# Filter tables in full rows spread on chip, multiplies off GpSimd, and a larger filter piece in a spectral and feed-forward mix on one core

## The chip, the cores and the metric

The kernel runs on one core of a Trainium2 chip. The metric is the device time of one execution in microseconds (us). Beside timed runs there is one execution taken with the hardware profiler, whose trace gives start and length of each instruction. TensorE (PE) multiplies matrices, VectorE (DVE) and ScalarE (ACT) work on elements and read TensorE's results from PSUM, GpSimd (POOL) is a further engine for element work in SBUF, and SyncE (SP) issues most DMA transfers, in the order of its queue.

## The reference

```python
# x: (1, 2048, 512) bf16; w_r, w_i: (2048, 257) bf16; w1: (512, 1792); w2: (1792, 512)
g = sigmoid((x * gate_w).sum(-1, keepdims=True))
X = jnp.fft.rfft2(x.astype(jnp.float32), axes=(-2, -1))
a = jnp.fft.irfft2(X * (w_r + 1j * w_i), s=(2048, 512), axes=(-2, -1)).astype(jnp.bfloat16)
h = jnp.einsum("bsd,df->bsf", x, w1) + b1
sp = jnp.log1p(jnp.exp(-jnp.abs(h))) + jnp.where(h > 0, h, 0)
b = jnp.einsum("bsf,fd->bsd", h * jnp.tanh(sp), w2)
out = g * a + (1 - g) * b
```

The spectral half filters x in the frequency domain with a complex table; the feed-forward half is two matmuls with mish between them; a gate per row mixes them.

## The kernel before

Everything stays in SBUF, in large regions that are used several times (rA to rF, rW, rX). The spectral half goes through matmul steps over 16 tiles of x or 64 frequencies. Sums and differences of x (the butterflies `bf`, L648) go to rB; step `p` (L662, evacuated by `ep`) and step `d` (L673, evacuated by `ed` to rD) transform along rows and columns; y1 is written to a DRAM scratch in four parts (`s1w`) and read back in another layout as In in rE (`s1r`). Step `t` (L757) multiplies In with the constants M in eight groups q, and the evacuation `et` writes Y. The filter is then, for each group, the product of Y with the real table (`p1`, L772), the product of Y with its two halves of partitions exchanged (two DMA transfers `sa` and `sb` into a buffer z, one of three) with the imaginary table (`p2`, L775), and their sum (`ad`, L778). When all groups are done, the edge step (`e1`, L794, to `e3`) corrects one column. Step `it` (L830) with the constants G and step `id` (L869) transform back, with evacuations `eit` and `ey`; `ip` and `fin` bring the result to the output.

The feed-forward half works on four chunks of 512 rows: `mm1` (L890) takes x transposed (xT) and w1, `h` adds the bias (VectorE L897 or ScalarE L901 and L902), ScalarE applies exp, ln and tanh (L911 to L914), `mul` (L923) multiplies h with tanh in eight pieces a chunk, `mm2` (L939) multiplies with w2, and `o` (L953 or L956) scales by the gate. xT of tiles 0 to 3 is made by TensorE (`tr`, L635), that of tiles 4 to 15 by DMA transposes (L518).

The tables: for each of w_r and w_i the columns 0 to 128 are loaded straight into their place (`d` loads) and the columns 128 to 256 into a staging region in rA (`s` loads), each with three transfers, one of them over rows in reversed order. GpSimd copies the staged part column-reversed into the table (`rev`, L725, 32x2064 each, four a table). The real table is then copied to the other 64 partitions by a DMA (`wru`), the imaginary one negated to them by VectorE (L735).

What runs when is set before the launch: `_Graph.schedule` places each task by ready time, by the priority of its class in the table `KN`, and by an assumed cost of each engine, and so chooses the engine (GpSimd or VectorE for `mul`, p1, p2, ad; VectorE or ScalarE for evacuations). Each engine then executes its list strictly in order and waits on semaphores. TensorE's results go through three pairs of PSUM banks (pool `pr`) and two single ones (`mm2`).

Of the kernel before, what the change touches and what calls it, by code (L numbers as in the profile page):

```python
# [160 lines left out]
class _Task:  # L161
    __slots__ = ("name", "eng", "dur", "fn", "deps", "base", "sem", "semval", "idx", "sig", "start", "done",
                 "succ", "bl", "cls", "off", "prio", "xfer", "opts", "isdma", "bufs", "tab", "lat", "dur0")

# [862 lines left out]
```

## Time and profile before

| | us |
|---|---|
| median of 2 timed runs (lowest, highest) | 170.19 (169.14, 171.25) |
| the profiled execution | 170.5 |
| its span, first to last instruction | 168.8 |
| mean granted TensorE clock | 0.949 of full speed |
| chain that ended last, largest shares | VectorE 30%, SyncE's queue 24%, TensorE 20%, DMA 12% |
| first `t` matmul, first edge matmul | 86.27, 123.93 |

Times inside the span count from its first instruction. A row that groups instructions gives their number after an x; "idle before" is the time in which the engine stood still ahead of them, and the arrow names what ended it. A clock of 1.00 is 2.4 GHz and 0.50 is 1.2 GHz.

### The profile page before, as it was taken

The numbers are of one execution on the slowest core, as the hardware profiler recorded it, in microseconds if no ns is written. First come the engines' busy times: TensorE is split into PE (matmuls) and PEld (weight loads), VectorE is DVE, ScalarE is ACT, GpSimd is POOL, SyncE is SP. The second block draws the span as 40 slices with busy tenths as digits, with TensorE's granted clock in tenths as the row PEclk, the third lists the DMA queues.
The fourth block names the chain that finished last, engine by engine and source line by source line (L and its number), as shares of the span: only waits on it lengthen the run. The fifth ranks groups of instructions, "written<-read, shape, count | busy, mean of one in ns | idle before, by whom it ended". The sixth has DMA issues, their size and how long they took to land.

```text
span 168.8 us, 2313 instructions
## 1 busy us (share of the span) xinstructions
PE 134.8 (80%) x901; PEld 72.9 (43%) x901; DVE 138.3 (82%) x155; ACT 110.5 (65%) x75; POOL 58.8 (35%) x48
## 2 busy tenths in 40 slices
PE   4599999989108999857369969997058999999993
PEld 3454444574103565322136624342025658753362
DVE  1394846699995389399978999999997999999993
ACT  3337899999501999954369889699129999940000
POOL 3005000002995013997501547768900000390000
PEclk9999999999955799999999999999957999999999
DMA  5999546999999979999915525040000000000544
GB/s 134 331 396 243 116 70 154 357 116 101 102 159 396 294 190 243 118 250 371 402 52 130 132 62 124 14 108 9 0 0 0 0 4 0 0 0 0 188 162 153
DMA packets 31055, 23.98 MB, mean 142 GB/s; under 512 B 23940, under 2 KB 27908, under 8 KB 30596
## 3 DMA queue, kind: packets, MB, share of 16 engines
q1 hardware_dynamic: 30720, 23.60, 60.4%
q10 hardware_dynamic: 324, 0.23, 0.6%
q8 instruction: 7, 0.11, 0.3%
q14 instruction: 4, 0.03, 0.1%
HBM read 14.90 MB, written 4.19 MB: 113 GB/s over the span
## 4 chain that ended last, share of the span: by engine, by line
DVE 30%; SPq 24%; PE 20%; DMA 12%; issue 7%; POOL 5%; DVEq 0%; POOLq 0%
SPq L519 12%; PE ps L939 12%; SPq L518 12%; DMA rW<-rW 6%; DMA rW<-in_A_w_r_dram 5%; DVE tmp L775 5%; POOL rC L725 5%; DVE rA L772 4%; DVE hs L923 4%; DVE hs L897 4%; DVE rC L556 3%; PE ps L869 3%; DVE rA L778 2%; PE ps L830 2%; DVE rC L735 2%
## 5 line engine op out<-in xcount | busy, mean ns | idle before, releaser
L890 PE MATMUL ps<-rX,w_sb 128*128 128x512 bf16 x224 | 49.8, 379 | 6.2 <-DVE rD L897 3.8
L939 PE MATMUL ps<-w_sb,hs 128*128 128x512 bf16 (+1 forms) x182 | 42.0, 380 | 11.0 <-POOL hs L923 8.4
L890 PEld LDWEIGHTS ps<-rX,w_sb 128*128 128x128 bf16 x224 | 21.5, 98 | 32.5 <-DVE rD L897 4.3
L939 PEld LDWEIGHTS ps<-w_sb,hs 128*128 128x128 bf16 x182 | 17.7, 101 | 30.0 <-POOL hs L923 8.6
L897 DVE TENSOR_TENSOR hs<-ps,b1f 128x1024 bf16<-128x1024 f32 x16 | 19.2, 1217 | 8.4 <-PE ps L890 8.4
L914 ACT ACTIVATE uT<-uT 128x4096 bf16<-128x4096 bf16 (+1 forms) x8 | 25.5, 3190 | 0.1
L913 ACT ACTIVATE uT<-uT 128x4096 bf16<-128x4096 bf16 (+1 forms) x8 | 25.5, 3190 | 0.1
L923 POOL TENSOR_TENSOR hs<-hs,uT 128x768 bf16<-128x768 bf16 (+1 forms) x8 | 15.0, 1877 | 24.3 <-ACT uT L914 23.4
L911 ACT ACTIVATE uT<-hs 128x2048 bf16<-128x2048 bf16 (+1 forms) x12 | 20.3, 1695 | 2.8 <-DVE hs L897 1.8
L923 DVE TENSOR_TENSOR hs<-hs,uT 128x1024 bf16<-128x1024 bf16 (+1 forms) x16 | 19.8, 1294 | 2.8 <-ACT uT L914 2.8
L556 DVE CAST rC<-ps 128x1024 bf16<-128x1024 f32 x16 | 19.3, 1261 | 0.5 <-PE ps L869 0.3
L725 POOL TENSOR_SCALAR rW<-rA 32x2064 bf16<-32x2064 bf16 x4 | 8.0, 2002 | 25.6 <-DMA rA<-in_A_w_r_dram 25.3
L939 PE MATMUL ps<-w_sb,rD 128*128 128x512 bf16 x56 | 14.9, 415 | 0.1
L556 DVE CAST rD<-ps 128x1024 bf16<-128x1024 f32 x8 | 10.2, 1305 | 5.6 <-PE ps L673 5.6
L778 POOL TENSOR_TENSOR rA<-rA,tmp 128x512 bf16<-128x512 bf16 x9 | 10.8, 1197 | 7.6 <-DVE rA L778 3.1
L911 ACT ACTIVATE uT<-rD 128x2048 bf16<-128x2048 bf16 (+1 forms) x4 | 6.8, 1698 | 6.3 <-DVE rD L897 6.3
L953 ACT ACTIVATE rX<-ps,omg 128x512 bf16<-128x512 f32 x5 | 3.4, 686 | 10.7 <-PE ps L939 10.7
L956 DVE TENSOR_SCALAR rX<-ps,omg 128x512 bf16<-128x512 f32 (+1 forms) x12 | 8.3, 694 | 1.6 <-PE ps L939 1.6
L775 DVE TENSOR_TENSOR tmp<-tmp,rC 128x512 bf16<-128x512 bf16 x13 | 9.4, 768 | 0.0
L556 DVE CAST rF<-ps 128x1024 bf16<-128x1024 f32 x8 | 9.2, 1217 | 0.1
L648 DVE TENSOR_TENSOR rB<-rA 128x1024 bf16<-128x1024 bf16 (+2 forms) x9 | 4.8, 566 | 5.0 <-DMA rA<-in_A_x_dram 5.0
L939 PEld LDWEIGHTS ps<-w_sb,rD 128*128 128x128 bf16 x56 | 5.6, 104 | 6.3 <-issue 1.7
(82 smaller groups left out, 167.3 us busy)
## 6 DMA issues: line engine op xcount, KB each, us to landing
rF<-c_m SPq DMA_DIRECT2D x1, 2048.0 KB, 10.3
scr<-rD SPq DMA_DIRECT2D x4, 512.0 KB, 7.1
rE<-scr SPq DMA_DIRECT2D x4, 512.0 KB, 6.7
rB<-c_g SPq DMA_DIRECT2D x1, 2048.0 KB, 10.5
tmp<-rA SPq DMA_DIRECT2D x16, 128.0 KB, 2.3
out_dram<-rX SPq DMA_DIRECT2D x7, 256.0 KB, 2.0
rA<-in_A_x_dram SPq DMA_DIRECT2D x3, 512.0 KB, 9.2
w_sb<-in_B_w_dram SPq DMA_DIRECT2D x2, 768.0 KB, 8.8
```

The lines of the kernel that those rows point to most:

```text
L518: return e.dma_start(a, b, transpose=True)
L519: return e.dma_start(a, b)
L556: return e.tensor_copy(out=o(), in_=i())
L725: return e.tensor_scalar(out=dstv[base + 32:base + 64, 16 * h:16 * h + 16, 0:129], in0=sg[:, 16 * h:16 * h + 16, 128::-1], scalar1=1.0, sc ...
L775: return e.tensor_tensor(out=zh(z), in0=zh(z), in1=Wi[:, fa:fb, 0:128], op=ALU.mult)
L890: ins = e.matmul(bank(b, i), w1_sb[:, dt_, 128 * ft:128 * (ft + 1)], xT[:, c, dt_, :, :], start=(dt_ == 0), stop=(dt_ == 3))
L897: return e.tensor_tensor(out=hs[hb][:, ft:ft + 2, :], in0=pair(b).rearrange("p (f s) -> p f s", f=2), in1=b1f[:, ft:ft + 2].unsqueeze(2).t ...
L911: return e.activation(o, hsf[hb][:, 512 * a:512 * b_], fn_)
L913: return e.activation(o, o, fn_, bias=1.0)
L914: return e.activation(o, o, fn_)
L923: return e.tensor_tensor(out=v, in0=v, in1=uv_[:, a:b_, 128 * tl:128 * (tl + 1)], op=ALU.mult)
L939: ins = e.matmul(bank(b)[:, 0:hi - lo], hs[hb][:, ft, 128 * tl:128 * (tl + 1)], w2_sb[:, ft, lo:hi], start=(ft == 0), stop=(ft == NFT - 1))
```

## The change

The tables are loaded once each, with whole rows of 257 elements, into rE, right behind x and w1 on SyncE's queue, in two halves of 32 frequencies: per half one transfer with the rows in order (16 KB contiguous for each of 16 partitions) and one with the rows reversed. Sixteen copies of 32x2064 (straight or column-reversed) spread them to the tables, and four instructions duplicate or negate them to the other 64 partitions, half by half, in place of the DMA copy and the one negation. Since rE is also the place of In, the four reads of In now wait for the last copy. The regions rA, rC and rE change roles: Y stands in rC, the imaginary table and later yb in rA. x of tiles 4 to 7 is transposed by TensorE. The three filter operations work on a whole group (128x1024) instead of halves. The task graph now assumes that GpSimd and VectorE exclude each other for tasks marked `lock`; DMA costs are given in us for each transfer; and the priorities `KN` are all new, so the order on every engine is new as well.

```diff
-    tr=108.5, bf=114.2, pd=110.85, ..., b_mul=1.2, b_fil=-0.8, b_rev=25.2,
+    tr=69.1, bf=78.15, pd=123.1, ..., d_w=113.1, d_xt=84.15, d_w2=72.45, d_m=126.15,
...
+                    if oe == "pool" or (oe == "dve" and t.lock):
+                        e_ = max(e_, lk_free)
...
-        for t in range(4, NT):
-            ld(f"xt{t}", xT[:, t // 4, :, t % 4, :], xv[:, t, :], 128 * KB, rate=210e3, transpose=True, writes=[("xT", t)])
+        for ri, (src, nm) in enumerate(((A_w_r, "wr"), (A_w_i, "wi"))):
+            wv = src.rearrange("(q m) k -> q m k", m=128)
+            for fh in range(2):
+                sg = stg[64 * ri + 32 * fh:64 * ri + 32 * fh + 32]
+                c0_ = 1 - fh
+                parts = [(0, slice(0, 32), slice(32 * fh, 32 * fh + 32), 0.9),
+                         (1, slice(c0_, 32), slice(127, 96, -1) if fh == 0 else slice(96, 64, -1), 1.8)]
+                if fh == 0:
+                    parts.append((1, slice(0, 1), slice(64, 65), 0.1))
+                for j, (pm, fs, ms, us) in enumerate(parts):
+                    ld(f"{nm}{fh}s{j}", sg[pm:32:2, fs, :], wv[:, ms, :], us, cls="d_w", writes=[(nm, fh, "s", j)])
+        for t in range(xtp, NT):
+            ld(f"xt{t}", xT[:, t // 4, :, t % 4, :], xv[:, t, :], 0.64, cls="d_xt", transpose=True, writes=[("xT", t)])
...
-        for t in range(4):
+        for t in range(xtp):
...
-                dma(f"{nm}s{j}", sg[pm:32:2, fs, 0:129], wv[:, ms, 128:257], nb, "w", rate=160e3, deps=t_bf + t_tr, writes=[(nm + "s", j)])
...
-                dma(f"{nm}d{j}", dstv[base + pm:base + 32:2, fs, 0:129], wv[:, ms, 0:129], nb, "w", rate=160e3, deps=dp + t_bf + t_tr, reads=[nm + "p"],
...
-                dma(f"{nm}u", dstv[64:128], dstv[0:64], 64 * 16640, "w", rate=340e3, reads=rd, writes=[nm])
...
+                            i_ = sg[:, 16 * h:16 * h + 16, 0:129] if pt == 0 else sg[:, 16 * h:16 * h + 16, 256:127:-1]
+                            o_ = dstv[base + 32 * pt:base + 32 * pt + 32, f0 + 16 * h:f0 + 16 * h + 16, 0:129]
...
+                    if ri == 0:
+                        return e.tensor_copy(out=dstv[64:128, f0:f0 + 32, :], in_=dstv[0:64, f0:f0 + 32, :])
+                    return e.tensor_scalar(out=dstv[0:64, f0:f0 + 32, :], in0=dstv[64:128, f0:f0 + 32, :], scalar1=-1.0, scalar2=None, op0=ALU.mult)
...
+            dma(f"s1r{g}", rE[g:128:4, 0:8192], scr_r[32 * g:32 * g + 32, :], 1.5, reads=[("scr", g)], writes=[("In", g)], deps=t_mv)
...
-                o = lambda f: [("dve", dve2(512), f), ("pool", pool(512), f, "b_fil")]
+            o = lambda f: [("dve", dve2(1024), f), ("pool", pool(1024), f, "b_fil")]
...
-                    G.any(f"mul{c}_{fh}_{tl}", [("pool", pool(n), f_mul), ("dve", dve2(n), f_mul, "b_mul")], "mul", off=-0.02 * tl,
+                    G.any(f"mul{c}_{fh}_{tl}", [("dve", dve2(n), f_mul), ("pool", pool(n), f_mul, "b_mul")], "mul", lock=True, off=-0.02 * tl,
```

How the order moves is shown at three places, by the instructions of one engine in a row (line, operation, out<-in, shape, number). First SyncE's queue from M to the edge constants, before and after; `rF<-c_m` is M, `scr<-rD` the writes of y1, `rE<-scr` the reads of In, `rB<-c_g` G.

```order
L519 DMA rF<-c_m 128x8192
L519 DMA scr<-rD 128x16x128
L519 DMA rW<-rW 64x8320
L519 DMA rE<-scr 32x8192
L519 DMA scr<-rD 128x16x128 x2
L519 DMA rC<-in_A_w_i_dram 16x64x129
L519 DMA rC<-in_A_w_i_dram 16x63x129
L519 DMA rC<-in_A_w_i_dram 16x129
L519 DMA scr<-rD 128x16x128
L519 DMA rE<-scr 32x8192 x3
L519 DMA rB<-c_g 128x8192
L519 DMA rD<-c_edge 128x1024
```

```order
L524 DMA rF<-c_m 128x8192
L524 DMA scr<-rD 128x16x128
L523 DMA_TRANSPOSE rX<-in_A_x_dram 128x4x128 x2
L524 DMA scr<-rD 128x16x128
L523 DMA_TRANSPOSE rX<-in_A_x_dram 128x4x128 x5
L524 DMA scr<-rD 128x16x128
L524 DMA w_sb<-in_B_w_dram 128x8x512
L524 DMA w_sb<-in_B_w_dram 128x6x512
L524 DMA scr<-rD 128x16x128
L524 DMA rB<-c_g 128x8192
L524 DMA rD<-c_edge 128x1024
L524 DMA rE<-scr 32x8192 x4
```

The reads of In stood between and right behind the writes and ahead of G; now all four stand behind w2, G and the edge constants, with the transposes spread between the writes.

Second, GpSimd's list from the first table copy on, before and after (L725, L744 and L745 are table copies, L923 multiplies of the feed-forward half, `wsr` a small extract of the duplicated table).

```order
L725 TENSOR_SCALAR rW<-rA 32x16x129 x4
L923 TENSOR_TENSOR hs<-hs,uT 128x6x128 x2
L739 CAST wsr<-rW 128x64x2
L741 MEMSET rW 128x64
L713 MEMSET rC 128x64
L725 TENSOR_SCALAR rC<-rA 32x16x129 x4
L923 TENSOR_TENSOR hs<-hs,uT 128x8x128
L923 TENSOR_TENSOR hs<-hs,uT 128x6x128
L739 CAST wsi<-rC 128x64x2
L741 MEMSET rC 128x64
L923 TENSOR_TENSOR hs<-hs,uT 128x6x128
```

```order
L744 COPY rW<-rE 32x16x129 x2
L745 TENSOR_SCALAR rW<-rE 32x16x129 x2
L744 COPY rW<-rE 32x16x129 x2
L745 TENSOR_SCALAR rW<-rE 32x16x129 x2
L733 MEMSET rA 128x32
L744 COPY rA<-rE 32x16x129 x2
L761 CAST wsr<-rW 128x32x2
L764 MEMSET rW 128x32
L745 TENSOR_SCALAR rA<-rE 32x16x129
L761 CAST wsr<-rW 128x32x2
L764 MEMSET rW 128x32
L745 TENSOR_SCALAR rA<-rE 32x16x129
```

Ten multiplies of the whole list are gone from GpSimd; sixteen copies stand there in a row, broken by the extracts, for which it waits for VectorE's duplications.

Third, VectorE where the filter begins, before and after (L775 and L799 are `p2`, L772 and L796 `p1`, L778 and L802 `ad`; L948 is `mul`, L922 `h`, L981 `o`).

```order
L556 CAST rA<-ps 128x1024
L897 TENSOR_TENSOR rD<-ps,b1f 128x1024
L956 TENSOR_SCALAR rX<-ps,omg 128x512
L556 CAST rA<-ps 128x1024 x2
L775 TENSOR_TENSOR tmp<-tmp,rC 128x512 x4
L772 TENSOR_TENSOR rA<-rA,rW 128x512 x2
L778 TENSOR_TENSOR rA<-rA,tmp 128x512
L775 TENSOR_TENSOR tmp<-tmp,rC 128x512 x2
L772 TENSOR_TENSOR rA<-rA,rW 128x512
L778 TENSOR_TENSOR rA<-rA,tmp 128x512
L772 TENSOR_TENSOR rA<-rA,rW 128x512
L778 TENSOR_TENSOR rA<-rA,tmp 128x512
```

```order
L948 TENSOR_TENSOR hs<-hs,uT 128x8x128 x2
L922 TENSOR_TENSOR hs<-ps,b1f 128x1024
L948 TENSOR_TENSOR hs<-hs,uT 128x6x128 x4
L981 TENSOR_SCALAR rX<-ps,omg 128x512
L799 TENSOR_TENSOR tmp<-tmp,rA 128x1024
L796 TENSOR_TENSOR rC<-rC,rW 128x1024
L802 TENSOR_TENSOR rC<-rC,tmp 128x1024
L799 TENSOR_TENSOR tmp<-tmp,rA 128x1024
L796 TENSOR_TENSOR rC<-rC,rW 128x1024
L802 TENSOR_TENSOR rC<-rC,tmp 128x1024
```

The evacuations of t (`rA<-ps` before) have left VectorE here, chunk 1's multiplies now stand ahead of the filter, and each group's three operations follow each other on VectorE; in all 20 of the 24 are on VectorE and four on GpSimd, where before it were 32 and 16 of half the size.

## Rows read from the trace of the kernel before

**Rows 1.** The page, part 1: busy us (share of the span) xinstructions.
```profile
PE 134.8 (80%) x901; PEld 72.9 (43%) x901; DVE 138.3 (82%) x155; ACT 110.5 (65%) x75; POOL 58.8 (35%) x48
```

**Rows 2.** Windows: length, busy us (x) PE PEld DVE ACT POOL, PEclk, DMA, GB/s.
```profile
33.00:52.00 19.00, 9.66 (x140) 6.58 (x138) 18.70 (x20) 11.30 (x6) 10.34 (x6) 0.86 1.35 146
...
66.00:86.30 20.30, 12.63 (x57) 5.09 (x56) 17.26 (x11) 12.13 (x9) 14.98 (x10) 1.00 1.02 265
...
86.30:123.90 37.60, 28.44 (x180) 14.47 (x180) 35.59 (x46) 28.77 (x21) 22.30 (x18) 0.97 0.28 65
...
123.90:168.80 44.90, 41.20 (x279) 24.47 (x279) 40.17 (x51) 23.92 (x14) 5.89 (x3) 0.95 0.13 48
```

**Rows 3.** Timeline, 41 to 57 us, GpSimd, VectorE, TensorE: start, us, engine.
```profile
41.16 8.26 POOL L725 TENSOR_SCALAR rW<-rA 32x2064 bf16<-32x2064 bf16 x4 [25.34 <-DMA rA<-in_A_w_r_dram]
...
41.60 4.05 DVE L923 TENSOR_TENSOR hs<-hs,uT 128x768 bf16<-128x768 bf16 x2
...
49.59 3.35 POOL L923 TENSOR_TENSOR hs<-hs,uT 128x768 bf16<-128x768 bf16 x2 [0.17 <-DVE gcol L704]
...
51.28 5.30 PE L939 MATMUL ps<-w_sb,hs 128*128 128x512 bf16 x12 [8.44 <-POOL hs L923]
```

**Rows 4.** The instructions of L923: ns min/median/max, first and last start.
```profile
L923 DVE TENSOR_TENSOR rD<-rD,uT x6: 550/682/685, 123.7 to 128.4; 128x1024 bf16<-128x1024 bf16 x3, 128x768 bf16<-128x768 bf16 x3
```

**Rows 5.** Groups by shape (last: the page's): busy us, mean ns of one, idle before.
```profile
L775 DVE TENSOR_TENSOR tmp<-tmp,rC 128x512 bf16<-128x512 bf16 x13 | 9.4, 768 | 0.0
...
L772 DVE TENSOR_TENSOR rA<-rA,rW 128x512 bf16<-128x512 bf16 x12 | 7.9, 661 | 0.0
...
L778 DVE TENSOR_TENSOR rA<-rA,tmp 128x512 bf16<-128x512 bf16 x7 | 6.0, 851 | 0.2
...
L897 DVE TENSOR_TENSOR hs<-ps,b1f 128x1024 bf16<-128x1024 f32 x16 | 19.2, 1217 | 8.4 <-PE ps L890 8.4
...
L725 POOL TENSOR_SCALAR rW<-rA 32x2064 bf16<-32x2064 bf16 x4 | 8.0, 2002 | 25.6 <-DMA rA<-in_A_w_r_dram 25.3
...
L923 POOL TENSOR_TENSOR rD<-rD,uT 128x1024 bf16<-128x1024 bf16 x1 | 2.1, 2115 | 0.1
...
L559 ACT ACTIVATE rA<-ps 128x1024 bf16<-128x1024 f32 x5 | 4.9, 1025 | 0.6 <-PE ps L757 0.6
...
L913 ACT ACT_TABLE_LOAD x4 | 5.1, 1283 | 0.1
...
L914 ACT ACTIVATE uT<-uT 128x4096 bf16<-128x4096 bf16 (+1 forms) x8 | 25.5, 3190 | 0.1
```

**Rows 6.** Timeline of TensorE: first feed-forward matmuls, first t, edge step.
```profile
8.90 24.33 PE L890 MATMUL ps<-rX,w_sb 128*128 128x512 bf16 x112
...
86.27 0.61 PE L757 MATMUL ps<-rE,rF 128*128 128x128 bf16 x8 [1.57 <-DVE rD L897]
...
123.93 0.16 PE L794 MATMUL ps<-rA,rD 128*128 128x1 bf16 x1 [6.84 <-issue]
...
124.49 3.60 PE L939 MATMUL ps<-w_sb,rD 128*128 128x512 bf16 x8
```

**Rows 7.** The chain that ended last: start us, us, what.
```profile
51.45 10.96 DMA rW<-rW
...
77.83 3.65 DVE rC L735
```

**Rows 8.** Windows in the front, by what the DMA queue carried.
```profile
5.00:13.00 8.00, 6.13 (x46) 3.33 (x45) 5.25 (x9) 3.18 (x6) 0.00 (x0) 1.00 1.04 375
...
13.00:27.00 14.00, 14.00 (x66) 6.37 (x65) 7.74 (x8) 11.97 (x12) 2.12 (x1) 1.00 0.68 133
...
33.80:46.40 12.60, 8.13 (x126) 5.57 (x123) 12.60 (x13) 10.50 (x6) 5.08 (x3) 1.00 1.44 106
```

**Rows 9.** Timeline: GpSimd's first wait for x.
```profile
13.69 2.12 POOL L648 TENSOR_TENSOR rB<-rA 128x1024 bf16<-128x1024 bf16 x1 [11.52 <-DMA rA<-in_A_x_dram]
```

**Rows 10.** DMA: issues, KB each, median us from issue to landing.
```profile
scr<-rD SPq DMA_DIRECT2D x4, 512.0 KB, 7.1
```

More of the change, by code (lines that the diff above doesn't have):

```diff
@@ L184, in __init__, with add @@
         self.pools = pools
-    def add(self, name, eng, dur, fn, cls, reads=(), writes=(), deps=(), off=0.0, opts=None, lat=0.0, tab=None):
+    def add(self, name, eng, dur, fn, cls, reads=(), writes=(), deps=(), off=0.0, opts=None, lat=0.0, tab=None, lock=False):
         t = _Task(name, eng, dur, fn, cls, off)
-        t.lat, t.tab, t.opts = lat, tab, opts
+        t.lat, t.tab, t.opts, t.lock = lat, tab, opts, lock
         seen = set()
@@ L315, in schedule @@
             free[t.eng] = est + t.dur
+            if t.eng == "pool" or (t.eng == "dve" and t.lock):
+                lk_free = est + t.dur
             if t.isdma:
-                xs = max(est + t.dur + 1.1, dq_free)
+                xs = max(est + t.dur + 0.9, dq_free)
                 dq_free = xs + t.xfer
-                t.done = dq_free + 1.0
+                t.done = dq_free + 0.8
             else:
@@ L681, in _build @@
             t_s1w.append(dma(f"s1w{g}", scr_w[:, 16 * g:16 * g + 16, :], rD[:, 2048 * g:2048 * (g + 1)].rearrange("p (r k) -> p r k", k=128),
-                             512 * KB, rate=180e3, reads=[("y1", 4 * g + i) for i in range(4)], writes=[("scr", g)]))
-            dma(f"s1r{g}", rE[g:128:4, :], scr_r[32 * g:32 * g + 32, :], 512 * KB, rate=320e3, reads=[("scr", g)], writes=[("In", g)])
-        dma("edge", rD[:, 7168:8192], d_edge[:].rearrange("p c m -> p (c m)"), 256 * KB, "dlate", writes=["edge"], deps=t_s1w)
+                             2.4, reads=[("y1", 4 * g + i) for i in range(4)], writes=[("scr", g)]))
+        dma("edge", rD[:, 7168:8192], d_edge[:].rearrange("p c m -> p (c m)"), 0.7, "dlate", writes=["edge"], deps=t_s1w)
         gb = _Buf("mm2")
@@ new lines, in _build @@
+        t_mv = [G.last_w[("stg", fh, ri, pt, h)] for fh in (0, 1) for ri in (0, 1) for pt in (0, 1) for h in (0, 1)]
+        for g in range(4):
+            dma(f"s1r{g}", rE[g:128:4, 0:8192], scr_r[32 * g:32 * g + 32, :], 1.5, reads=[("scr", g)], writes=[("In", g)], deps=t_mv)
+        dma("ldM", rF[:], d_M[:].rearrange("p f n -> p (f n)"), 5.6, "d_m", off=-0.1, writes=["M"], deps=t_p[6:7])
+        dma("ldG", rB[:], d_G[:].rearrange("p f n -> p (f n)"), 5.6, "dlate", writes=["G"], deps=t_p + t_s1w)
@@ L747, in _build @@
         t_t, t_fil = [], []
-        revs = [G.last_w[(nm + "r", h)] for nm in ("wr", "wi") for h in range(4)]
         for q in range(8):
@@ new lines, in _build @@
+            rw = [(z, 0), (z, 1)]
+            o = lambda f: [("dve", dve2(1024), f), ("pool", pool(1024), f, "b_fil")]
+            t_fil.append(G.any(f"p1_{q}", o(f_p1), "fil", off=0.3, lock=True, reads=[("wr", fh), ("Y", q)] + rw, writes=[("Yh", q)]))
+            t_fil.append(G.any(f"p2_{q}", o(f_p2), "fil", off=0.4, lock=True, reads=[("wi", fh), z] + rw, writes=[(z, 2)]))
+            t_fil.append(G.any(f"ad_{q}", o(f_ad), "fil", off=0.5, lock=True, reads=[(z, 2), z], writes=[("Yh", q)]))
@@ L961, in _build @@
                     if t == NT - 1:
-                        dma(f"out{t}_{lo}", ov[:, t, lo:hi], bs[:, t, lo:hi], 64 * KB, reads=keys, is_out=True, queue="sp" if lo else "act")
+                        dma(f"out{t}_{lo}", ov[:, t, lo:hi], bs[:, t, lo:hi], 0.25, reads=keys, is_out=True, queue="sp" if lo else "act")
                 if t < merge:
```

169 lines of the change are left out of this document (85 added, 84 removed).

## The prediction

> **What bounds the kernel now.** I read the page's busy shares first, then the windows by stage, then the chain of waits, and last the timeline at the places where an engine stands still. VectorE is busy for 138.3 of 168.8 us and TensorE for 134.8 [rows 1], but not evenly. From 33 to 52 us VectorE has no gap (18.70 of 19) while TensorE works 9.66; from 66 to 86.3 TensorE works 12.63 of 20.3; from 86.3 to 123.9, the filter, VectorE is full (35.59 of 37.6); from there to the end both are nearly full [rows 2]. So the first three of these stages can give time back, and the last only what is taken out of VectorE's and TensorE's own lists.
>
> Two things fill VectorE in those stages that are not its own work. First, it is held by GpSimd: two 128x768 multiplies took 4.05 us while GpSimd copied 32x2064 blocks [rows 3], against 0.55 each undisturbed [rows 4]. In the filter the same shows as means of 768, 661 and 851 ns [rows 5] for 128x512 operations, half of the 682 ns 128x1024 ones [rows 4], so 23.3 us for 32 instructions that should need about 13. Second, TensorE waits for GpSimd in person: 8.44 us at 42.8 to 51.3, until a multiply that stood behind four table copies was done, and then 12 matmuls took 5.30 us [rows 3], 0.44 each, where 112 took 24.33 (0.217) [rows 6]: the lower of the two clock levels. The tables themselves are on the chain: a copy of one table from partition to partition took 10.96 us and a negation 3.65 on VectorE [rows 7].
>
> **The change, step by step.** The sums are made against the profiled execution: 170.5 us with a span of 168.8, so 1.7 around it; the median of the two timed runs is 170.19 (169.14 to 171.25).
>
> *Table loads.* Before, twelve loads of 258-byte runs (8192 runs, 2.1 MB) ran at 106 GB/s [rows 8], some 410 runs per us. After, 2048 runs of 514 bytes and 64 of 16 KB, the same 2.1 MB, stand right behind x and w1. By bytes at that rate they take 20 us; by runs, 5.2 us for the short ones and 2.8 for the long ones at the 375 GB/s of x and w1 [rows 8], together 8. I take 10, since the long rows are like the latter and the short ones twice as long as those measured. The Trainium skill (SBUF — State Buffer, Door 1: The DMA port swizzle) says that a transfer into 32 neighbouring partitions reaches 8 of 16 ports and measured 189 GB/s for it; by that, an estimate of 11 us; no run here shows ports. The hint speaks against the change (a full row is no use if only half the ports take it), and the sum would be the same within 1 us.
>
> *The DMA queue up to the t step.* x is in by 13.7 us [rows 9]. Then: tables 10 (8 to 20); eight transposes at 1.17 (twelve filled 13 to 27 us [rows 8]), 9.3, where before there were twelve; M, 2.1 MB at 375 GB/s, 5.6; four writes of y1 to DRAM, 1.4 (375 GB/s) to 5 each (their 256-byte runs at 410 per us), I take 3 because 7.1 us to landing [rows 10] is with others in the queue; w2 4.9. That is 55 us (47 to 73). Behind it, in the new order of the SyncE queue, come G, edge and only then the four reads of In: 5.6 + 0.7 + 5.6, and some 2 for issue and landing. In is ready at 69 us (61 to 87).
>
> *GpSimd's copies.* Sixteen instead of eight, at 2.00 [rows 5], from about 17 us (x and half a table in): 32 us, and twice it must wait for VectorE's duplication of the other half (it stands ahead in GpSimd's list). They end at about 57. The reads of In wait for them too, but later than the queue lets them go, so this costs nothing unless a copy takes far over 2 us. Half of them are plain copies, a form that the trace does not show; the nearest rows are the 0.97 ns per element of the reversed ones and the 2.07 of a GpSimd multiply [rows 5], so 2.0 to 4.3 us. I take 2.0, the same data movement without reversal.
>
> *VectorE in the front.* Up to chunk 0's multiplies it has 14 bias additions (1.22 [rows 5]), 7 casts of the same size, 10 butterflies (at most 0.68 like other 128x1024 operations, 6 in all), two duplications (half of the 3.65 us instruction: 1.1 to 1.8): 34.8 us, from 3.8 us on with some 3 us of waiting for x: 41.6. About five of the SBUF operations meet a copy and wait for 1 us on average: 46.6. ScalarE is no earlier: the last exp of chunk 0 waits for the seventh bias addition, VectorE's work until about 30, and then come that exp, an evacuation, two loads of ScalarE's function table (1.28) and four passes of 3.19 [rows 5]: 47 to 48. Then come eight multiplies; five meet the last five copies (2.0 each), three take 0.6: done at 58.4. Before, they were done at 52.9 (49.59 + 3.35 [rows 3]). So the change first loses 5 us here: the cover for what it takes off GpSimd is gone.
>
> *TensorE up to t.* Before, t starts at 86.27 [rows 6]. After, there stand between the multiplies and t 20 + 28 matmuls of mm2 and 36 of mm1: 84 x 0.217 = 18.2, and 0.4: 77.0. TensorE waits some 5 us before them; should the clock fall as it did after 8.44 us, 12 matmuls cost 2.7 more: 79.7. In is ready by then in the middle case. I take 79.5 (77 to 82): 6.8 us gained. As much feed-forward work is done by then as before (172 + 56 matmuls against 160 + 72).
>
> *From t to the end of the filter.* Before: 86.27 to 123.93 [rows 6], 37.7 us, with 35.6 of VectorE. Off VectorE's list go three evacuations of t (now all eight on ScalarE, at 1.03 [rows 5]): 3.7. The filter's 23.3 us become 20 operations of 0.68, 13.7: 9.6 less; four more are on GpSimd at 2.12 [rows 5]. Onto it come chunk 1's multiplies, all eight (4 x 0.68 + 4 x 0.55 = 4.9) or the later half (2.2), I take 3.5, and an o of 0.7. Seven bias additions stay. The four GpSimd operations can hold VectorE for 0 to 8.5 us; bias additions from PSUM run beside them, so 3. 35.6 - 3.7 - 9.6 + 3.5 + 0.7 + 3 = 29.5, with the 2 us of gaps of before 31.5; I take 32 (29 to 35). ScalarE's 28.77 us [rows 2] lose three pairs of bias additions and gain three evacuations and an o, about as much: just enough. The filter ends at 111.5.
>
> *From there to the end.* 44.9 us before [rows 2]. VectorE gets two more multiplies of chunk 2 and three of chunk 3 (1.2 + 1.9, less 1.2 for the one that waited for GpSimd) and loses four and a half o (3.3) and one evacuation (1.2): -2.6. TensorE stood 6.84 us before the edge step, and eight matmuls on the chain then took 3.60 instead of 1.74 [rows 6]; its wait becomes 2 to 3 us. Of these 4.5 I count a third, since ScalarE's list is as long as before (23.92 us [rows 2] without a gap, up to its last tanh 25 us after the filter), and its tanh of chunk 3 then ends at 137 and comes last together with VectorE: 43.4 (42 to 45).
>
> Sum: 79.5 + 32 + 43.4 + 1.7 = 156.6, so **157 us**. From the ends, 77 + 29 + 42 + 1.7 = 150 to 82 + 35 + 45 + 1.7 = 164.
>
> **The rivals.** (a) *In comes late.* G and edge now stand ahead of the reads, the tables ahead of the transposes. If table loads go by bytes and writes at 5 us, In is there at 87 and t at 87.5: 87.5 + 32 + 43.4 + 1.7 = 165. For it: 106 GB/s on the tables now; against: the runs are twice as long. 0.12. (b) *The lock moves to the front.* If each of the 14 SBUF operations of VectorE that lie in the time of the copies (four butterflies, two duplications, eight multiplies) pays what the two multiplies paid [rows 3], 1.5 us, or a whole copy more, it is 21 to 28 us where I count 12; with p and d late as well t starts at 88, the filter with its four GpSimd multiplies held for the full 8.5 us (36), 43.4, 1.7: 169, no change. The Trainium skill (SBUF — State Buffer, Who interferes with whom) has the rule: an operation with two SBUF inputs blocks for the whole of a GpSimd instruction that reads SBUF, whichever is first; the trace agrees [rows 3, 5]. Against it: GpSimd waits twice for VectorE, and 24 of VectorE's first 36 operations read PSUM. 0.12. (c) *Slower: the copies cost what GpSimd multiplies cost.* At 4.3 us a copy, sixteen from 17 us end at 90 with the waits, the reads land at 98, and t cannot start before: 98 + 32 + 43.4 + 1.7 = 175. It decides from about 4.0 us a copy, where t is at 93.4 and nothing is gained. For it: a new form; against: the reversed half is measured at 2.0. 0.06.
>
> **How the numbers follow.** The forecast has 0.70, and its own range is 150 to 164; with (a) 0.82 lies under 166. I give 150 to 167. A kernel of this length can be told from no change at about 2%, 3.4 us: faster needs under 166.8. Faster 0.82, same 0.12, slower 0.06.
>
> **What would show it.** Right: tables landed by 25 us; copies of 2 us from about 17; VectorE's SBUF operations at 2 us beside them and at 0.68 in the filter; first t between 77 and 82; first edge matmul near 111; no TensorE wait over 6 us. Wrong: In landing after 85, copies over 3 us, an idle VectorE in the filter (ScalarE's evacuations or the swap DMAs then set its pace), or a tail over 46 us because ScalarE's tanh of chunk 3 ends late.

## The result, and the profile after

The changed kernel takes **153.77 us** (median; 153.03 to 154.51) against 170.19 before: a ratio of 0.9035, 95% interval 0.873 to 0.934. 157 was predicted, with a range of 150 to 167. The profiled execution took 153.03 us with a span of 150.9. Medians and ratios below leave out executions more than 1.5% above the fastest of the same kernel; the profiled executions of the runs e6 (154.96 us) and e12 (162.21 us) are such ones.

The page of the changed kernel, busy time and chain:

```profile
PE 134.9 (89%) x917; PEld 72.8 (48%) x917; DVE 128.6 (85%) x150; ACT 116.3 (77%) x77; POOL 45.7 (30%) x39
...
PE 69%; DVE 19%; DMA 6%; issue 2%; ACT 2%; SPq 1%; DVEq 0%
```

TensorE's work is what it was [rows 1]; VectorE's fell by 9.7 us. The chain is now TensorE's own for 69%; before, two thirds of it lay on VectorE, the DMA queue and its landings. The windows by stage (length, busy us, granted clock, DMA share, GB/s) answer to [rows 2]:

```profile
45.80:58.90 13.10, 11.10 (x98) 5.13 (x98) 13.07 (x10) 6.05 (x3) 11.98 (x8) 0.87 0.82 221
58.90:76.05 17.15, 17.07 (x82) 7.88 (x83) 14.66 (x20) 16.94 (x9) 1.07 (x4) 1.00 0.66 261
76.05:105.50 29.45, 27.22 (x173) 13.96 (x171) 28.47 (x37) 28.93 (x20) 8.30 (x4) 1.00 0.34 82
105.50:150.90 45.40, 41.25 (x279) 24.14 (x279) 37.42 (x50) 30.15 (x20) 0.00 (x0) 0.96 0.13 47
```

The cuts are the first t matmul (76.05) and the first edge matmul (105.55):

```profile
76.05 0.61 PE L782 MATMUL ps<-rE,rF 128*128 128x128 bf16 x8
...
105.55 0.18 PE L818 MATMUL ps<-rC,rD 128*128 128x1 bf16 x1 [1.45 <-DVE rC L802]
...
106.98 3.57 PE L964 MATMUL ps<-w_sb,rD 128*128 128x512 bf16 x8 [0.99 <-DVE rD L948]
```

So the 17.9 us of span came from two places: 10.2 ahead of t (86.27 before [rows 6]) and 8.2 between t and the edge step (37.7 before). The tail got 0.5 longer. The timeline of the front, GpSimd, VectorE and TensorE (start, us; in brackets the wait and what ended it):

```profile
20.60 3.85 POOL L744 COPY rW<-rE 32x2064 bf16<-32x2064 bf16 x2 [18.27 <-DMA rE<-in_A_w_r_dram]
...
54.15 4.28 POOL L745 TENSOR_SCALAR rA<-rE 32x2064 bf16<-32x2064 bf16 x2
```

```profile
45.84 13.00 DVE L948 TENSOR_TENSOR hs<-hs,uT 128x1024 bf16<-128x1024 bf16 x8
```

```profile
46.38 1.74 PE L707 MATMUL ps<-gw_sb,rX 128*128 128x1 bf16 x64 [2.69 <-DMA rX<-in_A_x_dram]
...
54.89 1.89 PE L964 MATMUL ps<-w_sb,hs 128*128 128x512 bf16 x8 [0.74 <-DMA w_sb<-in_B_w_dram]
57.02 1.46 PE L964 MATMUL ps<-w_sb,hs 128*128 128x512 bf16 x6 [0.24 <-DMA w_sb<-in_B_w_dram]
58.98 3.20 PE L964 MATMUL ps<-w_sb,hs 128*128 128x512 bf16 x14 [0.51 <-DVE zcl L711]
```

Sixteen copies of 1.90 to 2.80 us (2.05 on average) run from 20.6 to 58.4, and beside the last five of them chunk 0's eight multiplies take 13.0 us instead of the 4.9 of undisturbed ones [rows 4]. L707 are the 64 matmuls of the gate; `zcl` is the gate's sum, which VectorE takes from PSUM behind the multiplies, and `ez`, further down, its exponential on ScalarE. TensorE's largest wait here is now 2.69 us, for xT, where it was 8.44 for GpSimd [rows 3].

### The profile page after: what moved, and what is told of

Same layout as the page of the kernel before. It is cut to its first block, busy times and chain, and to the rows that moved or that the text cites. A ratio compares the mean times of both kernels' runs of the same rounds, so it can differ in the third digit from the quotient of the medians.

```text
span 150.9 us, 2300 instructions
## 1 busy us (share of the span) xinstructions
PE 134.9 (89%) x917; PEld 72.8 (48%) x917; DVE 128.6 (85%) x150; ACT 116.3 (77%) x77; POOL 45.7 (30%) x39
## 4 chain that ended last, share of the span: by engine, by line
PE 69%; DVE 19%; DMA 6%; issue 2%; ACT 2%; SPq 1%; DVEq 0%
PE ps L964 30%; PE ps L915 26%; DVE hs L948 9%; DMA w_sb<-in_B_w_dram 4%; DVE hs L922 3%; PE ps L894 3%; PE ps L855 2%; PE ps L782 2%; DMA rE<-c_inv 2%; PE ps L990 2%; PE ps L688 2%; DVE rA L559 2%; DVE rB L663 1%; DVE rW L756 1%; PE ps L677 1%
## 5 line engine op out<-in xcount | busy, mean ns | idle before, releaser
L915 PE MATMUL ps<-rX,w_sb 128*128 128x512 bf16 x224 | 52.5, 388 | 1.7 <-DVE rE L880 0.8
L915 PEld LDWEIGHTS ps<-rX,w_sb 128*128 128x128 bf16 x224 | 21.7, 100 | 27.5 <-issue 2.3
L922 DVE TENSOR_TENSOR hs<-ps,b1f 128x1024 bf16<-128x1024 f32 x21 | 25.3, 1217 | 3.4 <-PE ps L915 3.2
L948 DVE TENSOR_TENSOR hs<-hs,uT 128x1024 bf16<-128x1024 bf16 (+1 forms) x24 | 22.0, 976 | 1.3 <-ACT uT L939 1.3
L562 ACT ACTIVATE rC<-ps 128x1024 bf16<-128x1024 f32 x14 | 14.0, 1022 | 1.7 <-PE ps L677 1.7
L978 ACT ACTIVATE rX<-ps,omg 128x512 bf16<-128x512 f32 (+1 forms) x8 | 5.3, 660 | 11.1 <-PE ps L964 11.1
L744 POOL COPY rW<-rE 32x2064 bf16<-32x2064 bf16 x4 | 7.8, 1959 | 18.6 <-DMA rE<-in_A_w_r_dram 18.3
L559 DVE CAST rA<-ps 128x1024 bf16<-128x1024 f32 x7 | 8.6, 1294 | 1.1 <-PE ps L894 1.1
L796 POOL TENSOR_TENSOR rC<-rC,rW 128x1024 bf16<-128x1024 bf16 x2 | 4.0, 2025 | 18.0 <-DMA tmp<-rC 18.0
L744 POOL COPY rA<-rE 32x2064 bf16<-32x2064 bf16 x4 | 9.3, 2319 | 0.4 <-POOL rA L733 0.3
L994 DVE SCALAR_TENSOR_TENSOR rX<-ps,gcol,rX 128x512 bf16<-128x512 f32 x12 | 8.3, 745 | 1.2 <-PE ps L990 1.1
L922 DVE TENSOR_TENSOR rD<-ps,b1f 128x1024 bf16<-128x1024 f32 x7 | 8.3, 1218 | 0.7 <-PE ps L915 0.7
L981 DVE TENSOR_SCALAR rX<-ps,omg 128x512 bf16<-128x512 f32 (+1 forms) x9 | 6.5, 719 | 2.0 <-PE ps L964 1.8
```

The lines of the kernel that those rows point to most:

```text
L559: return e.tensor_copy(out=o(), in_=i())
L562: return e.activation(o(), i(), AF.Copy)
L744: return e.tensor_copy(out=o_, in_=i_)
L915: ins = e.matmul(bank(b, i), w1_sb[:, dt_, 128 * ft:128 * (ft + 1)], xT[:, c, dt_, :, :], start=(dt_ == 0), stop=(dt_ == 3))
L922: return e.tensor_tensor(out=hs[hb][:, ft:ft + 2, :], in0=pair(b).rearrange("p (f s) -> p f s", f=2), in1=b1f[:, ft:ft + 2].unsqueeze(2).t ...
L948: return e.tensor_tensor(out=v, in0=v, in1=uv_[:, a:b_, 128 * tl:128 * (tl + 1)], op=ALU.mult)
```

## The experiments

Each line of this table is worked out from one profiled execution, cut as above at the first t and the first edge matmul; the last two columns are the median of the timed executions and the ratio to the kernel before, timed beside them. The interval of the changed kernel's own ratio is wide (two executions), so the runs are better compared with each other. And t moves from trace to trace: e1 is changed only behind t, and yet its t came 2.1 us later than the changed kernel's, so a difference of 2 us in t shows nothing by itself. The stage from t to the edge step is steadier: 29.5 to 29.7 in the seven traces of the changed kernel and its variants that leave it alone.

| run | t starts | t to edge | edge to end | median | ratio |
|---|---|---|---|---|---|
| before | 86.27 | 37.7 | 44.9 | 170.19 | 1 |
| after | 76.05 | 29.5 | 45.4 | 153.77 | 0.9035 |
| e1 half pieces | 78.15 | 31.5 | 45.3 | 155.59 | 0.9147 |
| e2 short runs | 82.31 | 29.5 | 45.4 | 159.14 | 0.9350 |
| e3 late copies | 76.83 | 29.5 | 45.4 | 153.61 | 0.9022 |
| e4 copies to ScalarE | 75.46 | 29.7 | 45.3 | 152.08 | 0.8937 |
| e5 w2 first | 78.14 | 29.5 | 44.6 | 153.77 | 0.9018 |
| e6 both (e4, e5) | 78.13 | 29.5 | 45.4 | 150.99 | 0.8862 |
| e7 multiplies back | 74.22 | 30.1 | 48.1 | 154.33 | 0.9064 |
| e8 xT by DMA | 76.60 | 38.7 | 63.0 | 179.30 | 1.0523 |
| e9 late copies, w2 first | 75.32 | 29.5 | 44.6 | 151.24 | 0.8875 |
| e10 before, filter on VectorE | 86.07 | 34.8 | 44.9 | 167.41 | 0.9822 |
| e11 before, multiplies on VectorE | 81.31 | 34.4 | 45.3 | 163.65 | 0.9635 |
| e12 old priorities | 85.84 | 29.1 | 45.6 | 160.01 | 0.9392 |

**e1: the filter in 128x512 pieces again.** Each of the 24 operations becomes two; the engines and their order stay.

```
-  return e.tensor_tensor(out=Y[:, fa:fb, :], in0=Y[:, fa:fb, :], in1=Wr[:, fa:fb, 0:128], op=ALU.mult)
+  for a in (fa, fa + 4):
+      ins = e.tensor_tensor(out=Y[:, a:a + 4, :], in0=Y[:, a:a + 4, :], in1=Wr[:, a:a + 4, 0:128], op=ALU.mult)
+  return ins
   ... (the other two products alike)
```

> The changed kernel with the order kept, each of the 24 filter operations written as two 128x512 instructions again. Theory (the filter is bound by VectorE's own list): 40 operations of 0.42 in place of 20 of 0.68 add 3.2 us, GpSimd's 8 of 1.15 add 0.7: first edge matmul at 108 to 109 instead of 105.6, time 156 to 157. Rival (the piece size costs nothing, the filter is set by ScalarE's evacuations of t and the swaps): edge at 105 to 106, time within 1 us of the changed kernel's 153.8.

Ratio 0.9147 (0.910 to 0.9195). The window from t to the edge step is 2.0 us longer (VectorE is busy in it for 30.67 us instead of 28.47), so VectorE's list sets it and the piece size is worth 2 of its 8.2 us. VectorE's groups of the filter in that window (busy us, mean ns):

```profile
L802 DVE TENSOR_TENSOR tmp<-tmp,rA 128x512 bf16<-128x512 bf16 x16 | 7.4, 504 | 0.0
L807 DVE TENSOR_TENSOR rC<-rC,tmp 128x512 bf16<-128x512 bf16 x12 | 6.2, 557 | 0.2
L797 DVE TENSOR_TENSOR rC<-rC,rW 128x512 bf16<-128x512 bf16 x12 | 4.5, 416 | 0.0
```

What is to be seen: the same shape cost 768, 851 and 661 ns before [rows 5]. The pieces became quicker without becoming larger. The spread in the kernel before (ns min/median/max) says where the means come from:

```profile
L772 DVE TENSOR_TENSOR rA<-rA,rW x12: 410/416/2330, 95.8 to 123.0; 128x512 bf16<-128x512 bf16 x12
L778 DVE TENSOR_TENSOR rA<-rA,tmp x7: 424/426/1741, 96.6 to 123.4; 128x512 bf16<-128x512 bf16 x7
```

The median operation took 416 to 426 ns there too; a few of up to 2.33 us raise the mean. e10 asks why.

**e2: each table load cut into two column halves** (runs of 256 or 258 bytes instead of 514 and 16 KB), order kept.

```
+ if cls == "d_w":
+     def two(e, _dst=dst, _src=src, t=t):
+         e.dma_start(_dst[:, :, 0:129], _src[:, :, 0:129]).then_inc(t.sem, 16)
+         return e.dma_start(_dst[:, :, 129:257], _src[:, :, 129:257])
```

> The changed kernel with the order kept, each table load cut by columns into two, so that all runs are 256 or 258 bytes, the same bytes. Theory (loads go by runs, some 410 per us): 8192 runs take 20 us in place of about 13; copies start 2 to 3 us later than 20.6, the gate's wait for xT (2.7 us) grows by 5 to 7, first t at 78 to 81, time 156 to 158. Rival (loads are off the path since GpSimd's 32 us of copies set the pace): copies start within 1 us of 20.6, time within 1 us of 153.8.

Ratio 0.935 (0.933 to 0.937): 5.4 us lost, more than the theory gave. GpSimd's first copy began only 1.2 us later (21.84), but SyncE was done with issuing the table loads at 29.1 instead of 15.7, and the transposes of x behind it came late:

```profile
49.35 1.86 PE L921 MATMUL ps<-rX,w_sb 128*128 128x512 bf16 x4 [5.28 <-DMA rX<-in_A_x_dram]
54.29 1.84 PE L713 MATMUL ps<-gw_sb,rX 128*128 128x1 bf16 x64 [3.08 <-DMA rX<-in_A_x_dram]
```

The long rows pay through what stands behind them in the queue, not through the tables themselves. The edit also makes 20 transfers out of 10, and the run does not tell the number of transfers from the length of the runs.

**e3 and e4: chunk 0's multiplies freed from the last copies.** In e3 the last four copies wait until the multiplies are done; in e4 two of them go to ScalarE, two wait.

```
+ cp = [T[n] for n in ("wim100", "wim101", "wim110", "wim111")]
+ cp[0].deps = [d for d in cp[0].deps if True] + [T["mul0_1_3"]]        # e3
+ for t in cp[:2]: ... t.eng, t.fn = "act", t.opts[2][2]                # e4
+ cp[2].deps = [...] + [T["wip1"], T["mul0_1_3"]]                       # e4
```

> The changed kernel with one more wait: the last four table copies on GpSimd start only when chunk 0's eight multiplies are done. Theory (the copies hold VectorE's multiplies, 13.0 us for eight that need 5, and this is on the path to the first t): multiplies done at 51 to 53, last copy at 60 to 62, reads of In landed at 73 to 75, which then comes last before t: first t at 73 to 75 instead of 76.2, time 151 to 153. Rival (the time of the multiplies is hidden behind the tables' path): t and time no earlier, 154 to 157, because the reads start 2 to 3 us later.

> As the run with the late copies, but two of the four last copies are on ScalarE between chunk 0's tanh and chunk 1's exp, where it waits. Theory: multiplies done at 51 to 53, copies done at 55 to 57, In landed at 68 to 70, first t at 69 to 71, time 148 to 150. Rival (the multiplies are hidden): 153 to 155, since ScalarE's exp of chunk 1 starts 2 us later.

The multiplies took 6.15 us (e3) and 6.16 (e4), with one copy beside them, instead of 13.00 with five: GpSimd's copies were what held them, by 1.7 us each. But t moved by +0.8 and -0.6 us, no more than it moves from trace to trace, and the ratios are 0.9022 (0.898 to 0.906) and 0.8937 (0.888 to 0.8995), so both theories fell. The rivals' reason, the tables' path, does not show either: t waited for no read of In. The multiplies and TensorE's timeline in e3 show what happened:

```profile
46.83 6.15 DVE L948 TENSOR_TENSOR hs<-hs,uT 128x1024 bf16<-128x1024 bf16 x8
```

```profile
48.58 1.85 PE L707 MATMUL ps<-gw_sb,rX 128*128 128x1 bf16 x64 [3.71 <-DMA rX<-in_A_x_dram]
50.67 5.87 PE L915 MATMUL ps<-rX,w_sb 128*128 128x512 bf16 x19 [0.24 <-DVE hs L948]
56.37 1.89 PE L964 MATMUL ps<-w_sb,hs 128*128 128x512 bf16 x8
58.48 4.48 PE L964 MATMUL ps<-w_sb,hs 128*128 128x512 bf16 x20 [0.22 <-DMA w_sb<-in_B_w_dram]
```

The multiplies were done at 53.0, but TensorE came to mm2 only at 56.4: it had waited for xT, then did 19 matmuls at 0.31 us each, and then met w2's second half. The 7 us that the lock takes from VectorE were hidden behind TensorE's own list, which starts with xT's landing.

**e5: w2 issued ahead of M.** M (first read at 76 us) and w2 (first read at 55) change places on SyncE's queue.

```
+ G.order["sp"] = so[:i] + [w2a, w2b] + so[i + 1:j] + [lm] + so[j + 2:]
```

> The changed kernel with one swap on SyncE's queue: the two w2 loads (1.75 MB, first needed by the chunk-0 mm2 matmuls at about 55 us) are issued where the load of M (2 MB, first needed by the first t matmul at about 76 us) was, at 21 us, and M is issued where w2 was, at 45 us. All else and every order on the other engines is kept. Theory (the chunk-0 multiplies, held to 13 us of VectorE by the copies, end the front at 58.9 us, and w2's landing is only 1 us of TensorE's waits behind them): TensorE loses the two waits of 0.74 and 0.24 us, still waits for zcl at 58.9, t stays at 75.5 to 76.2, time 152.5 to 154. Rival (w2 alone is what held TensorE): mm2 runs early, t 73 to 74, time 150 to 151. Rival on the other side (M at 45 us lands too late, or delays the y1 transfers behind it, In lands last): t at 78 or later, time 156.

Ratio 0.9018 (0.893 to 0.911), no difference. The two waits for w2 are gone, as expected; t did not keep its place, because in this execution xT landed 3.2 us later (TensorE's gate matmuls at 49.63, after a wait of 3.69; with the same swap 46.40 in e9) and the multiplies, still 13.00 us, began at 47.80. So t is at 78 as the last rival had it, but not for its reason: TensorE waited for no transfer behind xT. What t lost, the tail gave back in part (44.6, with the clock at 1.00).

**e6: e4 and e5 together.**

> Both edits: two of the last four copies on ScalarE and two on GpSimd behind the chunk-0 multiplies (which then end at about 53.5 us instead of 58.9), and the w2 loads issued ahead of M. Theory (two waits in a row: the multiplies, and w2 right behind them; each alone gives at most 1.7 us, both together give more than their sum): the chunk-0 mm2 starts by 53 to 54 us instead of 56.5, t at 72 to 73, time 148.5 to 150. Rival (the y1 write, read back as In, comes next): In lands at about 71.8, and t can't start before about 72 to 74, time 150 to 151.5, so only some of it is given. Rival (a third wait stands there, xT or the copies on ScalarE that delay the evacuations): 152 as with the copies alone.

Chunk 0's mm2 starts at 52.48 and is done by 58.7, as the theory said, and then TensorE waits for something else:

```profile
52.48 6.21 PE L964 MATMUL ps<-w_sb,hs 128*128 128x512 bf16 x28
62.45 8.72 PE L915 MATMUL ps<-rX,w_sb 128*128 128x512 bf16 x32 [3.76 <-DVE rD L922]
```

VectorE stood for 5.20 us until ez, the gate's exponential on ScalarE, was done at 59.8; ScalarE had the two copies (3.88 us) and two exp of chunk 1 ahead of it. So the rival "a third wait" was right for this trace. Two other executions took 150.93 and 151.04 us, ratio 0.8862 (0.876 to 0.896), an interval that lies under that of e3; whether they had the same wait is not known.

**e7: ten of the multiplies back on GpSimd**, at the places of their planned starts.

```
+ back = ["mul0_1_2", "mul0_1_3", "mul1_0_3", ...]
+ for t in ...: G.order["dve"].remove(t); t.eng = "pool"; p.insert(k, t)
```

> Ten of the 32 multiplies by uT, all of which the change put on VectorE, go back to GpSimd at the places where they stood by the plan (two between the copies, three behind the last copy, five in the tail); every other order is kept. Theory (the saving of the change in the front needs GpSimd free for the copies): GpSimd carries 2 x 1.65 us more before its last copy ends (about 61.5 us) and then 5.4 us of chunk-0 multiplies (2115 and 1632 ns each), so the chunk-0 mm2 waits until about 67 us instead of 58.9; t at about 83, time 159 to 162. Rival (VectorE is the bound and the copies, not the multiplies' engine, give the gain): VectorE gets 10 x 0.6 us back and the time stays within 152 to 155.

The theory fell: 0.9064 (0.8975 to 0.915), the rival's time. Its reason, that the multiplies' engine does not matter, is not shown by that, since in the kernel before it did matter (e11). Only two of the ten are chunk 0's, not five as the expectation counted; GpSimd did them ahead of its last five copies (at 49.12, 3.92 us for both), chunk 0's mm2 began at 53.75, and t at 74.22 is the earliest of all, by no more than t moves from trace to trace. The tail lost what the front won: 48.1, with waits of 2.09, 0.92 and 0.42 us for multiplies. With the copies ordered around them, a few multiplies on GpSimd in the front cost nothing; taking them off the tail is worth about 2.7 us by this trace.

**e8: xT of tiles 4 to 7 by the DMA transpose** (`xtp=4`).

> The changed kernel with xT of tiles 4 to 7 again by the DMA transpose, as before the change, not by TensorE (the planner orders the rest anew with the same priorities). Theory (the transposes on SyncE's queue, 1.5 to 7 us each as issued, stand ahead of w2 and the y1 write there): TensorE and the evacuations save about 1 us of work each, but xT and w2 land 6 us or more later; time 156 to 162. Rival (the DMA queue has room and TensorE, 89% busy, is the bound): 152 to 153.

1.0523 (1.038 to 1.067), slower than before the change. t started at 76.60, after one wait of 6.47 us for xT, but with less done ahead of it: 211 matmuls stand between t and the edge step instead of 173, some 8 us of feed-forward work more. Then come windows of 38.7 and 63.0. The planner, with priorities fitted to other work, left more of the feed-forward branch for the end; in the tail ScalarE is busy for 43.73 us instead of 30.15, and TensorE's 279 matmuls took 48.96 us at a clock of 0.84 instead of 41.25 at 0.96. The run does not price the transposes; it shows how far the plan hangs on them.

**e9: e3 and e5 together.**

> The changed kernel with the last four copies behind the chunk-0 multiplies on GpSimd and the w2 loads issued ahead of M; nothing is added to ScalarE, which in the run with copies on ScalarE held the gate's ez until 59.8 us. Theory (multiplies and w2 stood one behind the other): the chunk-0 mm2 starts at 52 to 53 us and ends by 59, TensorE goes on without a wait, t at 73 to 74; the copies end at about 61, s1r is issued by 62, In lands at 71 to 72, just ahead; time 150 to 151.5. Rival (the copies are now late and In lands last): In at 74 to 76, t at 76, time 153 to 154. Rival (another wait in front, the gate or the evacuations): TensorE idles between 59 and 66, t at 76, time 153 to 154.

With e6 the fastest of all: 151.24, ratio 0.8875 (0.883 to 0.892), whose interval lies wholly under that of e3. Its chain in the front, and TensorE's timeline:

```profile
42.24 1.27 SPq L523
43.51 0.04 issue
43.55 2.72 DMA rX<-in_A_x_dram
46.27 0.14 issue
46.40 1.80 PE ps L707 x64
```

```profile
46.40 1.80 PE L707 MATMUL ps<-gw_sb,rX 128*128 128x1 bf16 x64 [2.29 <-DMA rX<-in_A_x_dram]
48.07 7.34 PE L915 MATMUL ps<-rX,w_sb 128*128 128x512 bf16 x20
55.24 6.21 PE L964 MATMUL ps<-w_sb,hs 128*128 128x512 bf16 x28
61.29 7.07 PE L915 MATMUL ps<-rX,w_sb 128*128 128x512 bf16 x32
```

From xT's landing to t TensorE does not wait. What it lost instead is clock: after the wait of 2.29 us, 20 matmuls took 7.34 us, 0.37 each instead of 0.217, and the gate's 64 came before them. So t came at 75.3, not at 73 to 74, and the last link ahead of it is now SyncE's row of transposes. Part of the lead over the changed kernel is the tail's clock (1.00 against 0.96, 0.8 us).

**e10: the kernel before, with GpSimd's 16 filter operations on VectorE.**

```
+ for t in [t for t in p if t.cls == "fil" and t.name[:2] in ("p1", "p2", "ad")]:
+     ... p.remove(t); t.eng = "dve"; v.insert(sum(u.start <= t.start for u in v), t)
```

> The kernel before with the 16 filter operations that GpSimd did (of 128x512) put on VectorE at the place of their planned start; every other order is kept, nothing is left out. It asks where the 8 us of the filter's window (t to the first edge matmul, 37.7 us before, 29.3 after) came from. Theory (GpSimd running beside VectorE made VectorE's pieces slow: 768, 661 and 851 ns before, 504, 416 and 557 ns in the run of the changed kernel with 128x512 pieces): 48 pieces at the undisturbed means are 23.6 us, the 32 disturbed ones of before were 23.3, so the window stays at 36 to 39 us though VectorE does half as much again; time 168 to 172. Rival (the pieces are as slow as they are, VectorE is the bound and GpSimd's part was a help): 16 more at 661 to 851 ns are 12.6 us, window about 50, time 181 to 183.

Faster by 1.8%, more than the theory gave: 0.9822 (0.979 to 0.985). VectorE does half as many operations again and is done sooner; the groups in the window:

```profile
L772 DVE TENSOR_TENSOR rA<-rA,rW 128x512 bf16<-128x512 bf16 x16 | 7.8, 505 | 0.0
L775 DVE TENSOR_TENSOR tmp<-tmp,rC 128x512 bf16<-128x512 bf16 x16 | 7.4, 494 | 0.0
...
L778 DVE TENSOR_TENSOR rA<-rA,tmp 128x512 bf16<-128x512 bf16 x16 | 6.5, 417 | 0.1
```

48 operations in 21.7 us, where 32 took 23.3 [rows 5]. The median is 416 ns in all three groups, and single ones still take up to 1.85 us beside the two multiplies that GpSimd keeps in this stage. GpSimd's 18.5 us of help in the filter were worth less than nothing.

**e11: the kernel before, with all multiplies by uT on VectorE.** The same edit, for the tasks whose names begin with "mul".

> The kernel before with all multiplies by uT on VectorE (ten leave GpSimd), every other order kept. Theory (two things held the front before, the tables' way over DMA and GpSimd's multiplies; with one gone the other still stands): TensorE's wait of 8.44 us for the chunk-0 multiplies shrinks to 2 to 4, but In and the tables' packing come as late as before, t at 83 to 86, the two multiplies in the filter's window leave VectorE a little quicker; time 166 to 169.5. Rival (the multiplies alone held the front): t at 78 to 80, time 161 to 164. Rival (no gain, VectorE pays for it): 170 to 172.

0.9635 (0.956 to 0.971), 7 us and more than the theory gave. The first t comes at 81.31 although the loads of the tables on SyncE's queue stand where they stood (their last at 65.04 to 68.62, before 66.52 to 68.96), so in the kernel before the multiplies alone cost 5 us ahead of t, half of what the change gained there; in the changed kernel e7 found no such cost. The window lost 3.3 us as well: GpSimd no longer does two of them there, and of VectorE's three groups in the filter (768, 661 and 851 ns before [rows 5]) two became quicker:

```profile
L775 DVE TENSOR_TENSOR tmp<-tmp,rC 128x512 bf16<-128x512 bf16 x13 | 9.4, 765 | 0.0
...
L772 DVE TENSOR_TENSOR rA<-rA,rW 128x512 bf16<-128x512 bf16 x12 | 5.9, 502 | 0.0
L778 DVE TENSOR_TENSOR rA<-rA,tmp 128x512 bf16<-128x512 bf16 x7 | 4.6, 663 | 0.2
```

**e12: the changed kernel, planned with the priorities of the kernel before.**

> The changed kernel planned with the priorities of the kernel before (the four numbers that only the new tasks have are set near their neighbours): same work, another order on every engine. By the order, SyncE's queue issues all eight xT transposes in a row, then w2, M, and only then the four y1 writes. Theory (part of the gain is the order in which loads and copies come): the y1 writes and In come 5 to 12 us later, time 158 to 168. Rival (what counts is the work taken off GpSimd and the DMA queue): 153 to 156. Rival on the other side (the old order on the new work is worse than before): over 172.

0.9392 (0.930 to 0.949). t is as late as before the change (85.84), so the gain ahead of t needs the new order too; the profiled execution took 162.21 us and two others 159.19 and 160.82, so its t may be a little high. The window is short with the old priorities as well (29.1), but it holds less work than the changed kernel's: 162 matmuls instead of 173, 23.25 us of ScalarE instead of 28.93, and two filter operations on GpSimd instead of four. So a short window does not need the new priorities; how long it would be with the same work in it is not shown. SyncE sent the eight transposes, w2 and M in one row and then stood for 25.9 us over the four writes of y1, so the reads of In were issued at 65.7 instead of 59.5.

## Why the prediction was right, step by step

The total lies well inside its range, but by errors that cancel in part: t came 3.4 us early and the window was 2.5 us shorter than forecast, the tail 2.0 longer, and t and the tail lie outside their own ranges (77 to 82, 42 to 45).

*The table loads* were mis-sized: 10 us forecast, but the queue needed about 12 (168 GB/s from 15.7 to 28.0, with the first transpose in it), so that the tables were in some 3 us behind the 25 that the prediction named, and the first copy began at 20.6, not at 17. The 189 GB/s that the Trainium skill (SBUF — State Buffer, Door 1: The DMA port swizzle) measured for 32 neighbouring partitions gave an estimate of 11, nearer than mine; no run tells whether ports are the reason.

*GpSimd's copies and VectorE in the front* came out as worked out, in part by luck: the copies were done at 58.4 (57 forecast), having begun 3.6 us late and waited less between; the multiplies were done at 58.84 (58.4), having begun 0.8 us early and taken 13.0 us instead of 11.8. The lock behind that number is shown by e3, e4 and e9, where the same eight multiplies took 6.15 to 6.16 us with one copy beside them instead of five. The Trainium skill (SBUF — State Buffer, Who interferes with whom) has the rule that a VectorE operation with two SBUF inputs and a GpSimd instruction that reads SBUF exclude each other. These three runs and e10 agree with it, but that a copy cost VectorE 1.7 us, a little less than the 1.90 that it takes undisturbed.

*First t* came 3.4 us early, 76.05 against 79.5. The step that failed is the clock: 2.7 us were allowed for matmuls at the low level behind TensorE's wait, but the wait was cut into 2.69, 0.74, 0.24 and 0.51 us. The clock did fall behind the first of these (0.78 from 46.4 to 54.2), while TensorE had the multiplies to wait for anyway; from 58.9 on it was 1.00. The other 1 us: 14 of chunk 0's mm2 matmuls were done while the multiplies still ran, and 78 instead of 84 were left.

*The window to the edge step* was 29.5 us, 32 forecast. VectorE's 28.47 us of work were forecast as 29.5; its gaps were 1 us, not 2, and the rest was rounding up. GpSimd's four operations held VectorE for some 2 us, not for 3 (one sum took 2.42 us and one product 1.10, where the medians are 0.69 and 0.68). ScalarE was as full as VectorE (28.93 us), as the prediction had it.

*The tail* was forecast 1.5 us shorter and got 0.5 longer. VectorE lost 2.75 us there, as worked out (2.6), but TensorE's 41.25 us are what set its length, and they did not change. That step counted as gain a third of what TensorE lost in the wait ahead of the edge step and in the slow matmuls behind it. The wait did shrink, from 6.84 to 1.45 us, but it lies in the window; behind it stood one of 0.99, and the slow matmuls came all the same (eight in 3.57 us, 3.60 before [rows 6]). ScalarE's list was not as long as before, either: 30.15 us instead of 23.92. Its last tanh ended at 134.9 (137 forecast), but from there to the last matmul the chain that ends last is TensorE's.

*The rivals.* (a) In was there at about 71.8 us, an estimate (SyncE was done with its reads at 62.0, and they landed 9.8 us after issue in the median), 4 us ahead of t; it did not decide. (b) The lock did move to the front, 7 us of it, but TensorE was nearly as late for another reason, as e3 shows. (c) Copies at 2.05 us on average, not 4.3: fell.

The prediction counted larger pieces and an end to the lock in the filter in one term (9.6 us of VectorE). The runs part them: of the window's 8.2 us the pieces are 2 (e1). In the kernel before, taking GpSimd out of the filter gave 2.9 (e10), and taking its multiplies away 3.3 in the window and 5.0 ahead of t (e11). These parts were measured each by itself, in different kernels, so that they come near the whole shows little. What the table loads, xT by TensorE, and the move of three evacuations of t from VectorE to ScalarE give by themselves was not separated, beyond e2's 5.4 us for the form of the loads.

## What to carry to other kernels

Before giving a slow engine a share of element-wise work, compare the mean and the median time of the fast engine's same-shaped instructions with and without it: here 16 operations moved to GpSimd made VectorE's other 32 slower by more than they saved. When a held engine is set free and the time stays, look at what the waiting engine's own list starts with and where that stands in its queue (here xT and w2 on SyncE's): waits that stand one behind the other give little one at a time. And a planner's priorities fit one set of work; a run that changes the work and plans anew measures the plan as well.

## What the runs showed of the hardware

VectorE's bf16 products and sums of 128x512 took 417 to 505 ns on average with two GpSimd multiplies in the stage (e10) and 661 to 851 ns with eighteen GpSimd operations of the same kind in it (before). The median is 416 to 459 ns in both: most were not held at all, and a few by up to 1.9 us (the longest took 2.33). The last four table copies took 8.91 us beside chunk 0's multiplies (after) and 7.78 behind them (e3), while the multiplies went from 13.00 to 6.15 us: VectorE pays for most of it.

How long TensorE waits did not by itself tell whether the granted clock fell. With a wait of 0.91 us ahead of the gate's 64 matmuls (e4) it was 0.78 over 7.8 us from these on, with 2.29 us ahead of them (e9) 0.77 over 15 us; with 0.83 us ahead of them (e7), or no wait (e1, e6), it stayed at 1.00, and so it did behind a wait of 3.44 us in e1. In the tail of the changed kernel, waits of 1.45 and 0.99 us with only four small edge matmuls between them were followed by eight matmuls at 0.45 us each, the lower level; in e9, after waits of 1.45 and 0.98 us at the same place and with the same matmuls, eight took 1.90 us in all. What made the difference is open.
